# The first weights' loads and conversions between the strided and the local units, and the first matmuls in a written order

## The chip, the cores and the metric

The kernel runs on one core of a Trainium2 chip. The metric is the device time of one execution in microseconds (us); less is better. A core has a matrix engine (PE, with its weight loads PEld), a vector engine (DVE), a scalar engine (ACT), a general engine (POOL) and a sync engine (SP) that here only issues transfers. Each works through its own list of instructions in order and waits on semaphores for the others.

## The reference

```python
# q, k, v: (8 batches, 8 heads, 576 positions, 64)
rel = pos[:, None] - pos[None, :]
mask_local = (rel >= 0) & (rel < 32)                                      # heads 0 to 3
mask_strided = (rel >= 0) & (pos[None, :] % 32 == pos[:, None] % 32)      # heads 4 to 7
attn = softmax(where(mask, q @ k.T / 8, -1e9)) ; out = attn @ v
x = out.transpose(0, 2, 1, 3).reshape(4608, 512)
h = x @ w_in                    # (512, 2048), 64-bit input
return (h * cos(h)) @ w_out     # (2048, 512), 64-bit input
```

## The kernel before

The work has two phases. In the first, each of the eight batches goes through attention and then through `x @ w_in`; the hidden values go to DRAM (`h_all`). In the second, 144 tiles of 128x512 hidden values are read back, multiplied by their cosine and by `w_out`.

Attention of a batch is seven **units**: four strided ones (two for each pair of heads) and three local ones (192 positions of four heads). A unit loads its q and k and then its v, multiplies q and k into a PSUM bank (the scores), goes through a softmax (DVE: largest value, subtraction; ACT: exponential; DVE: sum, small addition, reciprocal; POOL: product with the reciprocal), is transposed (a strided unit by PE and a copy on ACT, a local one by DVE alone), and is multiplied by v. In the units of batch 0 the products of a local unit are split right away into a rounded part `x_hi` (ACT) and the rest `x_lo` (DVE); those of the strided units are collected in `x0` and split once all four are there, by ACT and POOL (`FirstOperands.split`). The tiles that batch 0 loads into are named `v`, those of the later batches `qk` and `v`.

`x @ w_in` of batch 0 is eight `FirstBlock`s, one for each 256 columns. Each has eight products of six 128x288 matmuls, handed out to seven slots. A product with the strided half of x needs `x_hi`/`x_lo` of `x0` and the first two slots of the first block (18 matmuls) need nothing else; the third slot needs the local half. The weights come as 64-bit numbers in two 512 KB transfers for each block (`land`, tile `raw`, three buffers). `to_float32` makes them 32-bit with two instructions on ACT and two on DVE, and `split` makes the two parts with one on ACT and one on POOL (tile `w`). The later blocks' conversions are handed out over the slots.

What sets the order: SP issues all loads but the constants. PE's instructions are chained in the order in which the program writes them (`in_turn`); in the prologue of the kernel before, that chain is not used and the scheduler places PE's instructions. On the other engines the scheduler orders what is ready by its own reckoning, within what `order` demands. `PROLOGUE` lists by step which units (0 to 3 strided, 4 to 6 local, of batch 0) go one stage further. After each of the first steps come a few matmuls of no use (`keep_busy`, 128x512, 31 in all), whose number is in `BUSY`; ten of them stand after the products of unit 3. The first block's weights are converted from step 6 on, the second block's after the whole prologue. The weight loads come after the loads of batch 0's seven units (`units first`).

After the prologue the loop over slots runs: a product, then the attention of the next batch (`burst`), whose scores all use one PSUM bank, `acc0`. So the scores of the next unit wait until DVE has read the last ones.

Of the kernel before, what the change touches and what calls it, by code (L numbers as in the profile page):

```python
# [13 lines left out]
F32 = mybir.dt.float32  # L14
# [8 lines left out]
B, H, S, D = 8, 8, 576, 64  # L23
# [47 lines left out]

PROLOGUE = ((0,), (1,), (2,), (3,), (0, 4), (1, 0, 5), (2, 1, 6), (3, 2), (4, 4), (3,), (5, 5), (6, 6))
BUSY = (9, 2, 2, 2, 2, 2, 2, 10)

# [8 lines left out]
def attention_cos_ffn(ctx, tc, qkl, vl, qkvs, w_in, w_out, eye, eye16, mask_l0, mask_l, mask_s, out):  # L83
# [47 lines left out]
    def with_product(begun):  # L131
        if turn is not None:
            order(begun, turn, "with this product")

    def land(cv, src):
        raw = cv.tile([P, 512, 2], I32, name="raw", bufs=3)
        load = nc.sync.dma_start(out=raw.rearrange("p n w -> p (n w)"), in_=src)
        if len(loads) == UNITS:
            order(load, loads[-1], "units first")
        return raw  # L140
# [62 lines left out]
    class Attention:  # L203
        def __init__(self, stack):
            self.plain = True
# [11 lines left out]
        def banks(self, plain, scores, transposed, products, second):  # L217
            self.plain = plain
            self.scores, self.transposed, self.products, self.second = (
                itertools.cycle(kind) for kind in (scores, transposed, products, second)  # L220
            )

        def pe(self, mm):
            self.last = mm
            return mm if self.plain else in_turn(mm)

# [4 lines left out]
        def score_bank(self, b, mask):  # L231
            if b == 0:
                bank = self.bank(self.scores)
                n, w = mask.shape[1:]
                self.pe(nc.tensor.matmul(
                    bank[:, :n * w].rearrange("p (t w) -> p t w", w=w), ident16, mask, start=True, stop=False,
                    skip_group_check=True,
                ))
# [43 lines left out]
        def local(self, b, u):  # L282
            qk, v = self.inputs(b, QKL)
            loads.append(nc.sync.dma_start(out=qk[:, :QKL], in_=qkl[b, u]))
            nc.sync.dma_start(out=v[:, :VL], in_=vl[b, u])
            q_t = qk[:, :2 * LQ].rearrange("p (h q) -> p h q", h=2)
# [5 lines left out]
            def score(t, c):  # L292
                p, j = divmod(c, 2)
                self.scored = self.pe(nc.tensor.matmul(  # L294
                    s_ps[quarter_of(c), t * KW:(t + 1) * KW], q_t[half(j), p, QB * t:QB * (t + 1)],
                    k_t[half(j), p, QB * t:QB * t + KW], start=b > 0, stop=True, skip_group_check=True,
                ))
# [10 lines left out]
            def product(m, c):  # L308
                p, j = divmod(c, 2)
                lo, hi = max(m - 1, 0), min(m + 1, LU)  # L310
                at = m * KW - QB if m else 0
                self.pe(nc.tensor.matmul(  # L312
                    a_ps[p][half(j), lo * QB:hi * QB], v_t[quarter_of(c), m], pt[quarter_of(c), at:at + (hi - lo) * QB],
# [20 lines left out]
        def strided(self, b, p, u):  # L334
            real = min(SU, NG - SU * u)
            qk, v = self.inputs(b, QS + KS)
            spare = self.spare
            loads.append(nc.sync.dma_start(out=qk[:, :QS + KS], in_=qkvs[b, p, u, :, :QS + KS]))
            nc.sync.dma_start(out=v[:, :real * D], in_=qkvs[b, p, u, :, QS + KS:QS + KS + real * D])
            q_t = qk[:, :QS].rearrange("p (t q) -> p t q", q=GB)  # L340
# [5 lines left out]
            def score(t, i):  # L346
                self.scored = self.pe(nc.tensor.matmul(
                    s_ps[half(1 - i, GB), t * GB:(t + 1) * GB], q_t[half(i), t], k_t[half(i), t],
# [14 lines left out]
            for t in range(0, SU, 2):  # L363
                self.pe(nc.tensor.transpose(  # L364
                    t_ps[:, t * GP:(t + 2) * GP], pn[:, t:t + 2].rearrange("p t k -> p (t k)"), ident
                ))
# [8 lines left out]
            def product(t, j):  # L375
                at = (t ^ 1) * GB
                self.pe(nc.tensor.matmul(  # L377
                    a_ps[half(j), t * GB:(t + 1) * GB], v_t[half(j, GB), t], pt[half(j, GB), at:at + GB], start=True,
# [237 lines left out]
    with ExitStack() as phase:  # L616
# [18 lines left out]
        acc = [(ps, f"acc{i}") for i in range(3)]  # L635
        att.banks(True, (m,), (o,), (acc[1], acc[2]), (acc[0], o))
        operands[0] = FirstOperands()
# [3 lines left out]

        def keep_busy(bank, n, after):
            for _ in range(n):
                mm = nc.tensor.matmul(
                    bank, warm, warm.unsqueeze(1).broadcast_to([P, 4, P]), start=True, stop=True
                )
                if after is not None:
                    order(mm, after, "in its place")
                after = mm
# [18 lines left out]
        att.banks(False, (acc[0],), (acc[1],), (acc[2],), (acc[1],))  # L668

# [173 lines left out]
```

## Time and profile before

| | |
|---|---|
| median of 3 runs | 884.25 us (882.93 to 885.15) |
| the profiled execution | 883.67 us |
| its span | 881.9 us |
| PE busy | 869.3 us (99%) |
| DVE, ACT, POOL busy | 562.3, 530.1, 398.2 us |
| first product of `x @ w_in` | 29.75 us into the span |
| from then on PE waits | 2.7 us in all up to 130 us |

A row of the timeline gives the start in us from the start of the span, the duration in us, engine, line, operation, what is written and read, and how many instructions the row takes together. In brackets stands how long the engine had been idle before, and what ended that. The granted clock is a share of TensorE's 2.4 GHz; 0.5 is the lower of its two levels, 1.2 GHz.

### The profile page before, as it was taken

What the parts mean: (1) busy time and instruction counts of PE and PEld (TensorE: products, weight loads), DVE (VectorE), ACT (ScalarE), POOL (GpSimd) and SP (SyncE); (2) the same over time, 40 slices, a digit from 0 to 9 for tenths busy, and PEclk for the clock granted to TensorE, in tenths of its full rate; (3) what the DMA queues carried; (4) which work ended last, traced back from release to release, by engine and by line L of the source; (5) the groups of instructions that cost most, each with busy time, mean ns of one, the idle gap of its engine ahead of it and who ended that gap; (6) DMA issues with size and microseconds to landing.
All of it is one profiled execution on the core that took longest, in us unless ns stands there. A gap on an engine that the chain in (4) does not pass through costs nothing.

```text
span 881.9 us, 21351 instructions
## 1 busy us (share of the span) xinstructions
PE 869.3 (99%) x8439; PEld 775.9 (88%) x8439; DVE 562.3 (64%) x966; ACT 530.1 (60%) x1020; POOL 398.2 (45%) x341
## 2 busy tenths in 40 slices
PE   8999999999999999999999999999999999999998
PEld 5799899999999999999999888888888888888886
DVE  5778655767576675676425666666666666666662
ACT  3776544435445463454457777777777777777772
POOL 2578974316024051151355444444444444444442
PEclk9999999999999999999999999999999999999999
DMA  9697444565556556643285434343434344444431
GB/s 333 206 294 259 141 147 158 196 220 191 195 188 234 198 196 201 197 159 122 101 278 188 135 96 144 100 145 101 144 100 141 112 129 120 128 119 121 131 109 48
DMA packets 70516, 143.83 MB, mean 163 GB/s; under 512 B 8208, under 2 KB 15632, under 8 KB 70416
## 3 DMA queue, kind: packets, MB, share of 16 engines
q1 hardware_dynamic: 69696, 142.24, 50.2%
q8 instruction: 66, 1.08, 0.5%
q14 instruction: 34, 0.28, 0.1%
q10 hardware_dynamic: 720, 0.23, 0.1%
HBM read 91.06 MB, written 51.38 MB: 162 GB/s over the span
## 4 chain that ended last, share of the span: by engine, by line
PE 52%; DMA 2%; ACT 1%; POOL 1%; DVE 0%; issue 0%; POOLq 0%; ACTq 0%
PE acc L602 44%; PE m L511 4%; PE n L511 2%; DMA both<-w_all 2%; PE o L511 1%; POOL w L160 1%; PE acc L312 0%; PE acc L377 0%; ACT w L159 0%; ACT r L585 0%; DVE r L586 0%; PE acc L294 0%; ACT r L587 0%; ACT L587 0%; PE acc L364 0%
## 5 line engine op out<-in xcount | busy, mean ns | idle before, releaser
L160 POOL TENSOR_TENSOR g_lo<-r,g_hi 128x512 fp32r<-128x512 f32 x144 | 186.3, 1294 | 205.2 <-ACT g_hi L159 201.0
L602 PE MATMUL acc<-w,g_hi 128*128 128x512 f32 x720 | 221.6, 389 | 0.0
L591 DVE TENSOR_TENSOR r<-r,h_in 128x512 f32<-128x512 f32 x144 | 151.0, 1049 | 103.9 <-ACT r L587 103.6
L602 PEld LDWEIGHTS acc<-w,g_hi 128*128 128x128 f32 x720 | 135.2, 188 | 28.1
L602 PE MATMUL acc<-w,g_lo 128*128 128x512 f32 x360 | 140.0, 389 | 0.0
L585 ACT ACTIVATE r<-h_in 128x512 int32<-128x512 f32 x144 | 91.1, 633 | 77.0 <-POOL g_lo L160 76.3
L602 PE MATMUL acc<-v,g_hi 128*128 128x512 f32 x432 | 133.0, 389 | 0.0
L587 ACT ACTIVATE r<-r,quarter 128x512 f32<-128x512 f32 x144 | 104.4, 725 | 23.1 <-DVE r L586 22.9
L586 DVE SCALAR_TENSOR_TENSOR r<-r,h_in 128x512 f32<-128x512 int32 x144 | 101.7, 707 | 22.4 <-ACT r L585 11.1
L511 PE MATMUL m<-x_hi,w 128*128 128x288 f32 x448 | 109.8, 300 | 1.9 <-DVE h L529 1.5
L511 PE MATMUL m<-x_hi,v 128*128 128x288 f32 x448 | 109.1, 298 | 1.0 <-ACT m L519 0.9
L602 PEld LDWEIGHTS acc<-v,g_hi 128*128 128x128 f32 x432 | 81.0, 188 | 16.8
L159 ACT CAST g_hi<-r 128x512 fp32r<-128x512 f32 x144 | 89.6, 623 | 2.4 <-PE acc L602 1.2
L602 PE MATMUL acc<-v,g_lo 128*128 128x512 f32 x216 | 84.0, 389 | 0.0
L511 PEld LDWEIGHTS m<-x_hi,w 128*128 128x128 f32 x448 | 78.0, 188 | 3.8 <-DVE h L529 2.2
L511 PEld LDWEIGHTS m<-x_hi,v 128*128 128x128 f32 x448 | 78.0, 188 | 2.5 <-ACT m L519 1.7
L602 PEld LDWEIGHTS acc<-w,g_lo 128*128 128x128 f32 x360 | 67.5, 188 | 14.0
L519 ACT COPY m<-m 128x288 f32<-128x288 f32 x112 | 44.5, 397 | 57.3 <-PE m L511 52.3
L511 PE MATMUL m<-x_lo,w 128*128 128x288 f32 x224 | 66.1, 295 | 0.0
L511 PE MATMUL m<-x_lo,v 128*128 128x288 f32 x224 | 66.1, 295 | 0.0
L264 POOL TENSOR_TENSOR pn_s<-e_sb,z 128x324 f32<-128x324 f32 x28 | 21.2, 756 | 93.3 <-DVE z L262 72.2
L264 POOL TENSOR_TENSOR e_sb<-e_sb,z 128x384 f32<-128x384 f32 x24 | 20.9, 872 | 92.1 <-DVE z L262 81.6
(115 smaller groups left out, 1704.5 us busy)
## 6 DMA issues: line engine op xcount, KB each, us to landing
h_all<-h SPq DMA_DIRECT2D x128, 288.0 KB, 2.7
h_in<-h_all SPq DMA_DIRECT2D x144, 256.0 KB, 2.7
out<-o SPq DMA_DIRECT2D x36, 256.0 KB, 2.4
qk<-in_qkvs SPq DMA_DIRECT2D x28, 324.0 KB, 4.0
qk<-in_qkl SPq DMA_DIRECT2D x21, 416.0 KB, 3.9
raw<-in_w_in SPq DMA_DIRECT2D x16, 512.0 KB, 4.7
raw<-in_w_out SPq DMA_DIRECT2D x16, 512.0 KB, 4.3
v<-in_vl SPq DMA_DIRECT2D x24, 224.0 KB, 3.1
```

Of the source, the lines that this page charges most:

```text
L159: with_product(nc.scalar.copy(out=hi, in_=x))
L160: nc.gpsimd.tensor_tensor(out=lo, in0=x, in1=hi.bitcast(F32), op=ALU.subtract)
L264: nc.gpsimd.tensor_tensor(out=pn, in0=e, in1=z[:, :n].unsqueeze(2).broadcast_to([P, n, w]), op=ALU.mult)
L511: in_turn(nc.tensor.matmul(bank, a[:, c * P:(c + 1) * P], y[:, c], start=first and i == 0, stop=i == len(ops) - 1, skip_group_check=True,))
L519: nc.scalar.copy(out=t, in_=self.bank[name[0]])
L585: with_product(nc.scalar.activation(out=k, in_=h, func=AF.Copy, scale=1.0 / (2.0 * math.pi), bias=0.25))
L586: nc.vector.scalar_tensor_tensor(out=r, in0=k, scalar=-2.0 * math.pi, in1=h, op0=ALU.mult, op1=ALU.add)
L587: sin = nc.scalar.activation(out=r, in_=r, func=AF.Sin, bias=quarter)
L591: nc.vector.tensor_tensor(out=r, in0=r, in1=h, op=ALU.mult)
L602: in_turn(nc.tensor.matmul(acc[t], g[:, at], w, start=(f == 0 and i == 0), stop=(f == NFC - 1 and i == 2)))
```

## The change

The weight loads of the first block are put right behind the loads of the strided units, and the loads of the local units behind those: each of the first fourteen loads of units and the first four of weights is ordered behind the last one of these. The loads of batch 1 aren't part of that chain. The conversions of both blocks are stepped through by hand in the prologue. PE's prologue is one written list: Zn stands for n matmuls of no use (27 in all), a digit for the next stage of that unit, W and V with 0 or 1 for the next step of the first and second block's weights, X for the split of `x0`, P0 and P1 for the first two slots of the first block. These now stand among the local units' products, and all of PE's prologue is chained in that order.

```diff
-PROLOGUE = ((0,), (1,), (2,), (3,), (0, 4), (1, 0, 5), (2, 1, 6), (3, 2), (4, 4), (3,), (5, 5), (6, 6))
-BUSY = (9, 2, 2, 2, 2, 2, 2, 10)
+PROLOGUE = (
+    "Z9 0 Z2 1 Z2 2 Z2 3 W0 W1 Z2 0 Z2 1 0 Z2 W0 2 1 W0 W1 4 Z1 3 2 W1 5 Z2 3 X 6 Z3 V0 V1 4 4 P0 5 5 P1 6 6"
+)
...
+    def queued(load, b):
+        if b == 0:
+            if loads:
+                order(load, loads[-1], "in turn")
+            loads.append(load)
+
     def land(cv, src):
         raw = cv.tile([P, 512, 2], I32, name="raw", bufs=3)
         load = nc.sync.dma_start(out=raw.rearrange("p n w -> p (n w)"), in_=src)
-        if len(loads) == UNITS:
-            order(load, loads[-1], "units first")
+        if loads:
+            order(load, loads[-1], "in turn")
+        if len(loads) < 2 * UNITS + 4:
+            loads.append(load)
         return raw
...
-        def pe(self, mm):
-            self.last = mm
-            return mm if self.plain else in_turn(mm)
...
         def local(self, b, u):
             qk, v = self.inputs(b, QKL)
-            loads.append(nc.sync.dma_start(out=qk[:, :QKL], in_=qkl[b, u]))
-            nc.sync.dma_start(out=v[:, :VL], in_=vl[b, u])
+            for load in (
+                nc.sync.dma_start(out=qk[:, :QKL], in_=qkl[b, u]), nc.sync.dma_start(out=v[:, :VL], in_=vl[b, u])
+            ):
+                queued(load, b)
...
-        att.banks(True, (m,), (o,), (acc[1], acc[2]), (acc[0], o))
+        att.banks((m,), (o,), (acc[1], acc[2]), (o, acc[0]))
...
-        keep_busy(spare, BUSY[0], None)
-        for k, staged in enumerate(PROLOGUE):
-            for i in staged:
-                stage(units[i])
-            if k + 2 < len(BUSY):
-                keep_busy(spare, BUSY[k + 1], att.scored)
-            if k == 6:
-                turn = att.scored
-                for i in range(2):
-                    list(input_weights(cv, 0, i))
-            if k == 9:
-                keep_busy(pools["m"].tile([P, 512], F32, name="m"), BUSY[-1], att.last)
-                turn = att.last
+        first = [FirstBlock(f) for f in range(NF)]
+        early = {kind: [input_weights(cv, f, i) for i in range(2)] for f, kind in enumerate("WV")}
+        for word in PROLOGUE.split():
+            kind, n = word[0], int(word[1:] or 0)
+            if kind == "Z":
+                for _ in range(n):
+                    in_turn(nc.tensor.matmul(
+                        spare, warm, warm.unsqueeze(1).broadcast_to([P, 4, P]), start=True, stop=True
+                    ))
+            elif kind in early:
+                next(early[kind][n])
+            elif kind == "X":
                 operands[0].split(0)
                 operands[0].split(1)
-        for i in range(2):
-            list(input_weights(cv, 1, i))
+            elif kind == "P":
+                first[0].products(n)
+            else:
+                stage(units[int(word)])
...
         for f in range(NF):
-            first = FirstBlock(f)
-            for slot in range(STEP):
-                plan[STEP * f + slot] = partial(first.products, slot)
+            for slot in range(0 if f else 2, STEP):
+                plan[STEP * f + slot] = partial(first[f].products, slot)
...
+        for i in range(2):
+            for step in early["V"][i]:
+                pass
```

The lists of instructions that result differ at three places. The first is SP's list behind the eight loads of the strided units (`in_qkvs` into `v`). `in_qkl` and `in_vl` into `v` are batch 0's local units, `raw` are weights, whatever goes into `qk` and the `v` after it is batch 1. Before:

```order
L284 DMA v_263<-in_qkl 128x832
L285 DMA v_263<-in_vl 128x448
L284 DMA v_327<-in_qkl 128x832
L285 DMA v_327<-in_vl 128x448
L284 DMA v_389<-in_qkl 128x832
L285 DMA v_389<-in_vl 128x448
L137 DMA raw_430<-in_w_in 128x1024
L137 DMA raw_441<-in_w_in 128x1024
L137 DMA raw_601<-in_w_in 128x1024
L338 DMA qk_651<-in_qkvs 128x648
```

The same place of SP's list with the change:

```order
L146 DMA raw_255<-in_w_in 128x1024
L146 DMA raw_257<-in_w_in 128x1024
L346 DMA qk_646<-in_qkvs 128x648
L347 DMA v_647<-in_qkvs 128x384
L346 DMA qk_728<-in_qkvs 128x648
L347 DMA v_729<-in_qkvs 128x320
L290 DMA qk_806<-in_qkl 128x832
L290 DMA v_807<-in_vl 128x448
L290 DMA v_325<-in_qkl 128x832
L290 DMA v_325<-in_vl 128x448
L290 DMA v_390<-in_qkl 128x832
L290 DMA v_390<-in_vl 128x448
```

The two weight loads and six loads of batch 1's first three units now stand ahead of the first local load of batch 0, which was the ninth of SP's transfers and is the seventeenth; the third local unit's loads and the second block's weights follow.

The second place is DVE's list at the softmaxes of the three local units. Before, the second one begins while the first is under way (`mx_293`, `e_sb_292` and `z_297` are the first unit's, `mx_357`, `e_sb_356` and `z_361` the second's, `mx_419` the third's):

```order
L252 TENSOR_REDUCE mx_293<-m_266 128x6
L261 TENSOR_SCALAR z_250<-z_250 128x6
L253 TENSOR_TENSOR e_sb_292<-m_266,mx_293 128x384
L262 RECIPROCAL z_250<-z_250 128x6
L260 TENSOR_REDUCE z_297<-e_sb_292 128x6
L261 TENSOR_SCALAR z_297<-z_297 128x6
L252 TENSOR_REDUCE mx_357<-m_330 128x6
L262 RECIPROCAL z_297<-z_297 128x6
L253 TENSOR_TENSOR e_sb_356<-m_330,mx_357 128x384
L302 STREAM_TRANSPOSE pt_l_302<-e_sb_292 128x384
L260 TENSOR_REDUCE z_361<-e_sb_356 128x6
L252 TENSOR_REDUCE mx_419<-m_392 128x6
```

The same place of DVE's list with the change (the first unit's instructions and the second's):

```order
L257 TENSOR_REDUCE mx_355<-m_328 128x6
L258 TENSOR_TENSOR e_sb_354<-m_328,mx_355 128x384
L265 TENSOR_REDUCE z_359<-e_sb_354 128x6
L266 TENSOR_SCALAR z_359<-z_359 128x6
L267 RECIPROCAL z_359<-z_359 128x6
L309 STREAM_TRANSPOSE pt_l_364<-e_sb_354 128x384
L257 TENSOR_REDUCE mx_420<-m_393 128x6
L258 TENSOR_TENSOR e_sb_419<-m_393,mx_420 128x384
L265 TENSOR_REDUCE z_424<-e_sb_419 128x6
L266 TENSOR_SCALAR z_424<-z_424 128x6
L267 RECIPROCAL z_424<-z_424 128x6
L309 STREAM_TRANSPOSE pt_l_429<-e_sb_419 128x384
```

Each unit's six instructions now stand together, up to its transpose, and the third unit's six follow in the same way.

The third place is DVE's list with the change, behind the last `x_lo` of the local units and up to the subtraction of batch 1's first softmax. `n_624`/`v_623` and `n_632`/`v_623` are the conversions of the second block's weights:

```order
L162 SCALAR_TENSOR_TENSOR n_624<-raw_494,n_624 128x512
L165 SCALAR_TENSOR_TENSOR v_623<-raw_494,n_624 128x512
L333 TENSOR_TENSOR x_lo_130<-acc1_589,x_hi_129 128x192
L333 TENSOR_TENSOR x_lo_130<-o_590,x_hi_129 128x192
L162 SCALAR_TENSOR_TENSOR n_632<-raw_496,n_632 128x512
L260 TENSOR_TENSOR acc0_650<-acc0_650,ms_64 128x324
L165 SCALAR_TENSOR_TENSOR v_623<-raw_496,n_632 128x512
L261 TENSOR_REDUCE mx_665<-acc0_650 128x6
L262 TENSOR_TENSOR e_sb_664<-acc0_650,mx_665 128x324
```

Before, the same stretch of DVE's list, where `n_681`/`v_680` and `o_713` are the conversions of the third block's weights, and the second block's lie ahead of it:

```order
L326 TENSOR_TENSOR x_lo_130<-acc1_567,x_hi_129 128x192
L326 TENSOR_TENSOR x_lo_130<-acc0_568,x_hi_129 128x192
L151 SCALAR_TENSOR_TENSOR n_681<-raw_638,n_681 128x512
L255 TENSOR_TENSOR acc0_655<-acc0_655,ms_64 128x324
L154 SCALAR_TENSOR_TENSOR v_680<-raw_638,n_681 128x512
L151 SCALAR_TENSOR_TENSOR o_713<-raw_640,o_713 128x512
L256 TENSOR_REDUCE mx_670<-acc0_655 128x6
L489 COPY h_631<-m_630 128x288
L154 SCALAR_TENSOR_TENSOR v_680<-raw_640,o_713 128x512
L257 TENSOR_TENSOR e_sb_669<-acc0_655,mx_670 128x324
```

In this stretch the second block's four conversions take the place of the third block's; with the change the third block's four stand between the subtractions of batch 1's first and second softmax, twelve instructions apart from one subtraction to the next, where before there were seven.

## Rows read from the trace of the kernel before

**Rows 1.** The page's first part: busy time of each engine in us, share of the span, instructions.

```profile
PE 869.3 (99%) x8439; PEld 775.9 (88%) x8439; DVE 562.3 (64%) x966; ACT 530.1 (60%) x1020; POOL 398.2 (45%) x341
```

**Rows 2.** Waits of PE between 30 and 130 us: who waited for whom, us in total, times, longest.

```profile
PE acc L242 <- DVE x_lo L326: 1.2, 1, 1.2
PE n L511 <- ACT n L519: 1.1, 1, 1.1
```

**Rows 3.** The timeline of PE: matmuls of no use (L644), the first product of `x @ w_in` (L482 at 29.75), batch 1's scores (L242, L347, L294) and the products after them. The row at 34.69 is the first product with the local half, the one at 39.60 the first of the second block.

```profile
24.90 2.88 PE L644 MATMUL m<-warm 128*128 128x512 bf16 x10
...
29.75 0.40 PE L482 MATMUL m<-x_hi,w 128*128 128x288 f32 x1
...
34.69 0.40 PE L482 MATMUL m<-x_hi,w 128*128 128x288 f32 x1
...
38.88 0.80 PE L347 MATMUL acc<-qk 64*54 64x54 f32 x20
39.60 0.40 PE L482 MATMUL m<-x_hi,w 128*128 128x288 f32 x1
...
43.80 0.88 PE L294 MATMUL acc<-qk 64*32 64x64 f32 x48
```

**Rows 4.** The timeline of SP: when the first local load, the first of three weight loads and the first load of batch 1 were issued.

```profile
6.33 0.43 SPq L284 DMA_DIRECT2D v<-in_qkl  x1
...
9.73 2.47 SPq L137 DMA_DIRECT2D raw<-in_w_in  x3
12.50 0.33 SPq L338 DMA_DIRECT2D qk<-in_qkvs  x1
```

**Rows 5.** Transfers by issue, each row from the stretch in which one of those three was issued: count, KB, us from issue to landing.

```profile
v<-in_qkl SPq DMA_DIRECT2D x1, 416.0 KB, 5.5
...
raw<-in_w_in SPq DMA_DIRECT2D x1, 512.0 KB, 8.3
...
qk<-in_qkvs SPq DMA_DIRECT2D x1, 324.0 KB, 8.8
```

**Rows 6.** Transfers by issue between 0 and 70 us, for the sizes of the other loads (q and k of a strided unit of batch 0; v of a strided unit with six and with five groups; v of a local unit).

```profile
v<-in_vl SPq DMA_DIRECT2D x6, 224.0 KB, 5.9
...
v<-in_qkvs SPq DMA_DIRECT2D x4, 324.0 KB, 4.1
...
v<-in_qkvs SPq DMA_DIRECT2D x4, 192.0 KB, 4.1
v<-in_qkvs SPq DMA_DIRECT2D x4, 160.0 KB, 4.3
```

**Rows 7.** Two stretches from the start of the span: PE, PEld, DVE, ACT and POOL busy us (instructions), granted clock, share of the transfer engines, GB/s.

```profile
0.00:11.83 11.83, 10.32 (x111) 5.09 (x111) 5.20 (x16) 2.70 (x4) 3.12 (x11) 1.00 0.86 270
0.00:18.50 18.50, 16.92 (x269) 9.69 (x271) 9.36 (x29) 5.22 (x10) 6.07 (x15) 1.00 0.92 321
```

**Rows 8.** The timeline of DVE, ACT and POOL: the softmax of the first local unit and its transpose.

```profile
13.53 0.56 DVE L252 TENSOR_REDUCE mx<-m 128x6 f32<-128x384 f32 x1 [0.56 <-PE m L294]
...
14.19 0.56 DVE L253 TENSOR_TENSOR e_sb<-m,mx 128x384 f32<-128x384 f32 x1
...
14.78 0.52 ACT L258 ACTIVATE e_sb<-e_sb 128x384 f32<-128x384 f32 x1 [1.31 <-DVE e_sb L253]
...
15.34 0.55 DVE L260 TENSOR_REDUCE z<-e_sb 128x6 f32<-128x384 f32 x1 [0.49 <-ACT e_sb L258]
...
15.92 0.17 DVE L261 TENSOR_SCALAR z<-z 128x6 f32<-128x6 f32 x1
...
17.37 0.18 DVE L262 RECIPROCAL z<-z 128x6 f32<-128x6 f32 x1
...
17.70 0.83 POOL L264 TENSOR_TENSOR e_sb<-e_sb,z 128x384 f32<-128x384 f32 x1 [1.98 <-DVE z L262]
...
18.56 0.58 DVE L302 STREAM_TRANSPOSE pt_l<-e_sb 128x384 f32<-128x384 f32 x1 [0.44 <-POOL e_sb L264]
```

**Rows 9.** The timeline of POOL and DVE at the third local unit: a weight's second part on POOL, the small addition of the softmax on DVE.

```profile
22.87 1.28 POOL L160 TENSOR_TENSOR w<-v,w 128x512 fp32r<-128x512 f32 x1 [0.38 <-ACT w L159]
23.02 1.16 DVE L261 TENSOR_SCALAR z<-z 128x6 f32<-128x6 f32 x1
```

**Rows 10.** Two stretches, columns as in rows 7: the idle time of PE, and the time after it.

```profile
21.20:22.50 1.30, 0.00 (x2) 0.00 (x0) 1.30 (x4) 1.30 (x4) 0.83 (x1) 1.00 0.82 310
22.50:26.00 3.50, 3.50 (x64) 2.66 (x64) 3.47 (x8) 2.79 (x8) 2.11 (x2) 0.52 0.52 181
```

**Rows 11.** The timeline of ACT and DVE: an `x_lo` of a local unit (L326), two weight conversions in a row on ACT (L146, L150), a conversion on DVE (L151), and the subtractions of batch 1's first and second softmax (L257).

```profile
31.06 0.25 DVE L326 TENSOR_TENSOR x_lo<-acc,x_hi 128x96 fp32r<-128x96 f32 x1
...
34.16 0.63 ACT L146 ACTIVATE o<-raw 128x512 int32<-128x512 uint32 x1
34.32 0.69 DVE L151 SCALAR_TENSOR_TENSOR n<-raw,n 128x512 int32<-128x512 int32 x1 [0.73 <-ACT raw L150]
...
34.72 0.66 ACT L150 ACTIVATE raw<-raw 128x512 f32<-128x512 f32 x1
34.92 0.50 DVE L255 TENSOR_TENSOR acc<-acc,ms 128x324 f32<-128x324 f32 x1
...
37.88 0.48 DVE L257 TENSOR_TENSOR e_sb<-acc,mx 128x324 f32<-128x324 f32 x1
...
41.28 0.49 DVE L257 TENSOR_TENSOR e_sb<-acc,mx 128x324 f32<-128x324 f32 x1
```

More of the change, by code (lines that the diff above doesn't have):

```diff
@@ L204, in __init__ @@
         def __init__(self, stack):
-            self.plain = True
             self.ld, self.wk = (
@@ L215, in __init__, with banks @@
             self.kept, self.spare, self.x = None, None, {}
-        def banks(self, plain, scores, transposed, products, second):
-            self.plain = plain
+        def banks(self, scores, transposed, products, second):
             self.scores, self.transposed, self.products, self.second = (
@@ L234, in score_bank @@
                 n, w = mask.shape[1:]
-                self.pe(nc.tensor.matmul(
+                in_turn(nc.tensor.matmul(
                     bank[:, :n * w].rearrange("p (t w) -> p t w", w=w), ident16, mask, start=True, stop=False,
@@ L293, in score @@
                 p, j = divmod(c, 2)
-                self.scored = self.pe(nc.tensor.matmul(
+                in_turn(nc.tensor.matmul(
                     s_ps[quarter_of(c), t * KW:(t + 1) * KW], q_t[half(j), p, QB * t:QB * (t + 1)],
@@ L311, in product @@
                 at = m * KW - QB if m else 0
-                self.pe(nc.tensor.matmul(
+                in_turn(nc.tensor.matmul(
                     a_ps[p][half(j), lo * QB:hi * QB], v_t[quarter_of(c), m], pt[quarter_of(c), at:at + (hi - lo) * QB],
@@ L337, in strided @@
             spare = self.spare
-            loads.append(nc.sync.dma_start(out=qk[:, :QS + KS], in_=qkvs[b, p, u, :, :QS + KS]))
-            nc.sync.dma_start(out=v[:, :real * D], in_=qkvs[b, p, u, :, QS + KS:QS + KS + real * D])
+            for load in (
+                nc.sync.dma_start(out=qk[:, :QS + KS], in_=qkvs[b, p, u, :, :QS + KS]),
+                nc.sync.dma_start(out=v[:, :real * D], in_=qkvs[b, p, u, :, QS + KS:QS + KS + real * D]),
+            ):
+                queued(load, b)
             q_t = qk[:, :QS].rearrange("p (t q) -> p t q", q=GB)
@@ L346, in score @@
             def score(t, i):
-                self.scored = self.pe(nc.tensor.matmul(
+                in_turn(nc.tensor.matmul(
                     s_ps[half(1 - i, GB), t * GB:(t + 1) * GB], q_t[half(i), t], k_t[half(i), t],
@@ L363, in strided @@
             for t in range(0, SU, 2):
-                self.pe(nc.tensor.transpose(
+                in_turn(nc.tensor.transpose(
                     t_ps[:, t * GP:(t + 2) * GP], pn[:, t:t + 2].rearrange("p t k -> p (t k)"), ident
@@ L376, in product @@
                 at = (t ^ 1) * GB
-                self.pe(nc.tensor.matmul(
+                in_turn(nc.tensor.matmul(
                     a_ps[half(j), t * GB:(t + 1) * GB], v_t[half(j, GB), t], pt[half(j, GB), at:at + GB], start=True,
@@ L640, in attention_cos_ffn @@
         spare = ps.tile([P, 512], F32, name="acc0")
[L642 to L649, printed above, removed]
-        keep_busy(spare, BUSY[0], None)
-        for k, staged in enumerate(PROLOGUE):
-            for i in staged:
-                stage(units[i])
-            if k + 2 < len(BUSY):
-                keep_busy(spare, BUSY[k + 1], att.scored)
-            if k == 6:
-                turn = att.scored
-                for i in range(2):
-                    list(input_weights(cv, 0, i))
-            if k == 9:
-                keep_busy(pools["m"].tile([P, 512], F32, name="m"), BUSY[-1], att.last)
-                turn = att.last
+        first = [FirstBlock(f) for f in range(NF)]
[4 more added lines that the diff above has]
+                for _ in range(n):
+                    in_turn(nc.tensor.matmul(
+                        spare, warm, warm.unsqueeze(1).broadcast_to([P, 4, P]), start=True, stop=True
[3 more added lines that the diff above has]
+            elif kind == "X":
                 operands[0].split(0)
                 operands[0].split(1)
-        for i in range(2):
-            list(input_weights(cv, 1, i))
-        att.banks(False, (acc[0],), (acc[1],), (acc[2],), (acc[1],))
+            elif kind == "P":
+                first[0].products(n)
+            else:
+                stage(units[int(word)])
+        att.banks((acc[0],), (acc[1],), (acc[2],), (acc[1],))
         begun = np.interp(range(UNITS, B * UNITS + 3), [k for k, _ in KNOTS], [at for _, at in KNOTS])
```

## The prediction

> **What bounds the kernel now.** I read the busy times first: PE works for 99% of the span [rows 1]. Then its waits: from 30 to 130 us they are a couple of us [rows 2]. So once products follow one another, the end of the kernel moves with PE, and what the prologue gains or loses shows at the end one for one. No later stretch gives back time, since PE hardly waits there. What counts is how late PE is at fixed marks behind the prologue. In the timeline of PE these are [rows 3]: first product at 29.75, first product with the local half at 34.69, batch 1's second scores at 38.88, second block at 39.60, third scores at 43.80. Then I read what feeds those marks: SP's transfers, the local softmaxes, and the conversions on ACT and DVE.
>
> **What the change takes off PE's path.** The first two slots' 18 matmuls start at 29.75 and run at full clock in some 2.4 us; they now stand between the local units' products. The ten matmuls of no use behind unit 3's products (2.88 us [rows 3]) are gone. The first block's weights no longer compete with the local softmaxes. All of this gains only if PE isn't waiting there for something that now comes later, which is the next point.
>
> **The local units' loads.** In SP's list the first local q and k was the ninth transfer and is now the seventeenth: two weight loads and, outside the new chain, six loads of batch 1 stand ahead of it. In before it was issued at 6.33 and landed 5.5 us later, at 11.8 [rows 4, 5]. With the change there lie ahead of it four strided units, 4x324 + 2x192 + 2x160 = 2000 KB, 1024 KB of weights, and for batch 1 the same kinds of loads, 324 + 192 + 324 + 160 + 416 + 224 = 1640 KB [rows 5, 6]. With its own 416 KB that makes 5080 KB. When does so much land? In before, the 4432 KB up to the first weight load (2000, three local units of 640, and 512) were in at 9.73 + 8.3 = 18.0, and the 5780 KB up to batch 1's first q and k at 12.50 + 8.8 = 21.3 [rows 4, 5]; between these, 5080 KB come at 19.6. From below: at 11.83, 270 GB/s had moved 3.19 MB, 0.72 MB more than the 2.47 MB in order up to the tile that landed then. 5.20 + 0.72 MB had been moved by 18.5 (321 GB/s) [rows 7]. I take **19.2**, nearer the landing times, because as many transfers are under way there.
>
> **The local softmaxes.** DVE's list now has each local unit's six instructions in one piece, and the transpose at the end waits for POOL, so the second softmax can't begin before the first is through. One of them, without queueing, is [rows 8]: from 13.53 to the end of the small addition at 16.09 is 2.56; the reciprocal comes 0.03 later; from its start to the end of the transpose, 17.37 to 19.14, is 1.77. That is 4.36 us, and three in a row are 13.1. The first unit's scores take some 0.9 us (the 0.88 of the row at 43.80 [rows 3]). So the third unit is transposed at 19.2 + 0.9 + 13.1 = **33.2**. Loads of the second and third unit land within some 4 us of the first and are hidden behind this chain. So is the first block's conversion, ahead of it.
>
> Here PE still keeps up: `x0` can be split only once ACT has done the second unit's exponential (about 26.3), and POOL's two `x_lo` of it end near 31, so P0 runs from some 29.7 and the third unit's products end near 35.
>
> **The conversions behind them.** What PE meets next is a list that DVE and ACT have to work off. The subtraction of batch 1's first softmax must end before the second scores can use `acc0`. Ahead of it DVE now has the second block's four conversions, which in before were spread between 27 and 32 us. My sum: the last four `x_lo` and the casts between them need about 1.2 us (0.25 for one [rows 11], alternating with ACT), so ACT turns to the conversions at 34.4. Up to the one that DVE needs last (`n_632`) it has five conversions and a cast, which follow one another every 0.56 us (34.16 to 34.72 [rows 11]), and two small casts of 0.2: 3.9 us with a handover, to 38.3. Then DVE has the conversion (0.6, as from 34.32 to 34.92), the mask, another conversion, the reduction and the subtraction, 2.7 us in all: 41.0. In before that subtraction ended at 38.36 [rows 11] and PE came to the scores just then, 38.88. So PE is **2.2 us late** here (41.05 to 38.88).
>
> From there to the next subtraction DVE has twelve instructions where it had seven. Seven took 38.36 to 41.77, 3.4 us [rows 11]; four conversions more (0.6 each, less one copy shared) make 5.5, so that subtraction ends at 46.5. In before PE had 2.0 us to spare at this place (41.77 to 43.80); now it would come at 43.80 + 2.2 = 46.0 and waits **0.5 us** more. After that the two lists have the same work between marks, and no stall is left to add.
>
> **The clock.** PE is idle from about 16 to 19 us and again from about 26 to 29.7. In before, after 1.3 us of idle time and the many small matmuls around it, the granted clock was 0.52 for 3.5 us [rows 10], that is 1.2 GHz. I add 0.3 us for the first scores at that level; the rest of a low stretch is hidden, since DVE and ACT set the marks. The Trainium skill ("TensorE: Matmul & The Clock Gate", section on HAM oscillation) says that a wait for transfers between short pieces of matmuls brings the array to half its clock, and that the price is paid at each such wait; the trace agrees with 0.52 after the idle time, and by that rule both new waits would be followed by a low stretch, which would leave the sum as it is unless the second reaches past 37 us (rival 4).
>
> **Sum.** 2.2 + 0.5 + 0.3 = 3.0 us. My chains put almost nothing between engines, where rows show up to 0.1 us for each handover; for some of these I add 0.3. From the profiled execution's 883.67 that gives 887.0. It lay 0.6 under the median, so for the median I forecast 884.25 + 3.3 = **887.5**. A measurement of this kernel can tell 0.3% from no change, that is 2.65 us: the bounds are 881.6 and 886.9.
>
> A price that I leave out of the sum: in before, the small addition on DVE took 1.16 us instead of 0.17 while POOL made a weight's second part in 1.28, and ended with it [rows 8, 9]. The third softmax's addition falls at about 31.2, just behind POOL's `x_lo` of `x0`; if they meet, it costs up to 1.0. The Trainium skill ("SBUF — State Buffer", section on the two separate sides) calls the port pair of these two engines an exclusive lock, held for a whole instruction; the trace agrees with the 1.16, and by it the sum would be 4.3 instead of 3.3 if they meet.
>
> **The rivals.**
> 1. The forecast: local tiles land between 18.5 and 19.6, and the chains follow. Each us of landing moves the marks by one, so with the meeting on POOL at the upper end it gives 886.3 to 888.9. Chance 0.52.
> 2. The tiles land sooner but still behind batch 1's. Their load can't be issued before the eighth transfer ahead of it, a weight load, has landed at about 12.1 (2512 KB against the 2416 at 11.8); if it then takes 5.5 us as before, it lands at 17.6, and 3.3 - 1.6 leaves 886.0. For it: SP waits no longer than that. Against it: 8.3 to 8.8 us in the stretch when the engines are full [rows 5]. Chance 0.21.
> 3. Not slower: batch 1's loads cost the local ones nothing, because transfers under way share the engines. Then only 3440 KB count ahead and with them, which by the rows between 2416 at 11.8 and 4432 at 18.0 is 15.0; 4.2 us earlier than in the sum, that is 0.9 us faster than before, 883.4. The point from which it decides: a landing before 15.9. Against it: landing times in before follow the order of issue. Should the softmaxes overlap better too, it passes the bound of faster. Chance 0.14.
> 4. Much slower: the clock is still at 1.2 GHz when the 30 products of the first block's rest begin near 37 us. They take 4.2 us at full clock (34.69 to 38.88 [rows 3]) and would take 8.4; PE would come to the second scores at 45.4 instead of 41.0, and, less the 0.5 that it then no longer waits, the time is about 891. For it: the long idle times. Against it: PE has work from 29.7 on, and the low stretch of before lasted 3.5 us with PE busy. Chance 0.13.
>
> **How the numbers follow.** Slower by over 0.3% holds where the forecast's case lies above 886.9, some 0.43 of its 0.52, with rival 4's 0.13 and a little of rival 2: 0.58. Faster by over 0.3% is half of rival 3, 0.07. The rest, 0.35, is within. The range goes from 883.6 (rival 3's upper half and all of rival 2) to 890.6 (all but the larger part of rival 4), and leaves out less than 0.2.
>
> **What would show it.** In the profile after: the first local scores of batch 0 near 19 us, with PE idle for some 3 us ahead of them; three local transposes on DVE about 4.3 us apart, the last ending near 33; batch 1's second scores near 41 (before 38.9), waiting for DVE's subtraction; the second block near 41.8 (39.6) and the third scores near 46.5 (43.8); the granted clock low somewhere between 20 and 36. Local scores before 16 us would make the prediction wrong, and so would a second block near 39.6 in spite of late scores, which would mean that DVE and ACT work off their lists faster than I sum.

## The result, and the profile after

| | before | after |
|---|---|---|
| median, us | 884.35 (4 runs) | 889.5 (889.14 to 890.85, 4 runs) |
| profiled execution, us (its span) | 883.67 (881.9) | 889.18 (887.4) |

The ratio is 1.0063, with a 95% interval of 1.0045 to 1.008: the change costs 5.15 us by the medians, where 3.3 had been forecast. Of the profile I read the same marks on PE as before. Timeline of PE after; L301 at 18.64 are the first local scores, L492 the products of `x @ w_in`, L357 at 45.44 batch 1's second scores, L492 at 46.73 the second block, L301 at 51.43 the third scores:

```profile
18.64 0.87 PE L301 MATMUL m<-v 64*32 64x64 f32 x48 [1.95 <-DMA v<-in_qkl]
...
29.02 0.40 PE L492 MATMUL m<-x_lo,w 128*128 128x288 f32 x1 [1.48 <-POOL x_lo L171]
...
35.13 0.40 PE L492 MATMUL m<-x_hi,w 128*128 128x288 f32 x1
...
37.49 0.29 PE L492 MATMUL m<-x_hi,w 128*128 128x288 f32 x1
42.26 0.61 PE L492 MATMUL m<-x_hi,w 128*128 128x288 f32 x1 [4.48 <-DVE h L499]
...
45.44 1.36 PE L357 MATMUL acc<-qk 64*54 64x54 f32 x20
46.73 0.61 PE L492 MATMUL m<-x_hi,w 128*128 128x288 f32 x1
...
51.43 0.87 PE L301 MATMUL acc<-qk 64*32 64x64 f32 x48
```

Against [rows 3] the first product with the local half is only 0.44 us late (35.13 to 34.69). The second scores are 6.56 late, the second block 7.13, the third scores 7.63. So nearly all of the loss arises between 37.8 and 47.6 us, in two pieces: a stop of 4.48 us, and products that then take longer: the twelve up to the second scores need 3.18 us (42.26 to 45.44), where the run with the clock kept, below, has 1.80. The releaser named is DVE's copy of a finished bank into `h` (L499): the next product needs that bank. What held the copy, in the timelines of DVE, ACT and SP:

```profile
35.48 0.69 DVE L165 SCALAR_TENSOR_TENSOR v<-raw,n 128x512 int32<-128x512 int32 x1
...
39.51 0.49 DVE L262 TENSOR_TENSOR e_sb<-acc,mx 128x324 f32<-128x324 f32 x1
41.15 0.70 DVE L162 SCALAR_TENSOR_TENSOR o<-raw,o 128x512 int32<-128x512 int32 x1 [1.15 <-ACT raw L161]
41.76 0.45 DVE L499 COPY h<-m 128x288 f32<-128x288 f32 x1
```

```profile
39.93 0.62 ACT L157 ACTIVATE o<-raw 128x512 int32<-128x512 uint32 x1 [2.58 <-DMA raw<-in_w_in]
```

```profile
17.07 19.50 SPq L146 DMA_DIRECT2D raw<-in_w_in  x4
36.66 0.38 SPq L346 DMA_DIRECT2D qk<-in_qkvs  x1
```

and, between 10 and 45 us, what SP waited for (us in total, times, longest):

```profile
SPq L146 <- DVE v L165: 18.5, 4, 12.6
```

Read from the bottom: SP's fourth weight load in that row was issued at its end, 36.57, because it needed one of the three `raw` buffers: SP's weight loads waited 18.5 us in all for the conversions that read them, and the last of these to end before the issue is the second block's first, 35.48 to 36.17. ACT got the load 3.4 us later and worked from 39.93, DVE's conversion waited for ACT until 41.15, and the copy, one place behind it in DVE's list, ended at 42.21. DVE stood idle for 1.15 us with a copy behind it that was ready. In stretches of 2 us (columns as in [rows 7]):

```profile
17.00:19.00 2.00, 0.36 (x24) 0.36 (x28) 1.38 (x2) 0.89 (x4) 1.10 (x1) 1.00 1.06 417
27.00:29.00 2.00, 0.55 (x19) 0.29 (x9) 1.32 (x3) 0.23 (x1) 2.00 (x3) 1.00 0.00 0
39.00:41.00 2.00, 0.00 (x0) 0.00 (x0) 0.97 (x3) 1.07 (x2) 0.00 (x0) 1.00 0.86 313
41.00:43.00 2.00, 0.74 (x3) 0.74 (x4) 1.85 (x4) 2.00 (x6) 1.28 (x1) 0.51 0.35 143
43.00:45.00 2.00, 2.00 (x10) 2.00 (x10) 1.67 (x5) 0.70 (x3) 0.15 (x1) 0.50 0.55 152
45.00:47.00 2.00, 2.00 (x24) 1.62 (x23) 0.62 (x2) 1.70 (x4) 2.00 (x3) 0.50 1.15 299
47.00:49.00 2.00, 2.00 (x13) 2.00 (x14) 1.93 (x4) 0.00 (x0) 1.07 (x1) 0.78 0.75 248
```

The granted clock was 1.00 through the two early waits and fell to 0.50 (1.2 GHz) after the stop. By a later mark, the 21st store of an `h`, PE is 7.7 us late (issued at 127.61, before at 119.90); at the end of the span it is 5.5. The difference comes back where before itself waits: its listed waits of PE between 130 and 500 us add up to 3.1 us, those of after to 1.6. Not every kernel gets as much back: of the ten below, the five with the second block early gain 1.5 to 2.1 us between this mark and the end of the span, the other five from 0.3 us down to a loss of 0.9. Why they differ is open.

### The profile page after: what moved, and what is told of

It reads as the page before. It is cut to its first block, busy times and chain, and to the rows that moved or that the text cites. A ratio compares the mean times of both kernels' runs of the same rounds, so it can differ in the third digit from the quotient of the medians.

```text
span 887.4 us, 21340 instructions
## 1 busy us (share of the span) xinstructions
PE 869.7 (98%) x8435; PEld 776.9 (88%) x8435; DVE 567.4 (64%) x966; ACT 530.2 (60%) x1020; POOL 398.3 (45%) x341
## 4 chain that ended last, share of the span: by engine, by line
PE 91%; DVE 3%; DMA 3%; POOL 2%; ACT 1%; issue 1%; SPq 0%; POOLq 0%; ACTq 0%; DVEq 0%
PE acc L612 44%; PE m L521 19%; PE n L521 10%; PE m L492 5%; PE o L521 5%; PE acc L319 2%; PE acc L301 2%; PE acc L387 2%; PE acc L357 1%; DMA raw<-in_w_in 1%; PE acc L374 1%; DMA v<-in_qkl 1%; POOL x_lo L171 1%; DMA v<-in_qkvs 0%; POOL e_sb L269 0%
## 5 line engine op out<-in xcount | busy, mean ns | idle before, releaser
L521 PE MATMUL m<-x_hi,w 128*128 128x288 f32 x448 | 109.8, 300 | 2.1 <-DVE h L539 1.6
L492 PE MATMUL m<-x_hi,w 128*128 128x288 f32 x256 | 57.5, 308 | 4.5 <-DVE h L499 4.5
```

The source lines that it names most:

```text
L492: in_turn(nc.tensor.matmul(self.banks[i, j], a[:, c * P:(c + 1) * P], y[:, c], start=k == 0 and m == 0, stop=k == 1 and m == len(ops) - 1, ...
L521: in_turn(nc.tensor.matmul(bank, a[:, c * P:(c + 1) * P], y[:, c], start=first and i == 0, stop=i == len(ops) - 1, skip_group_check=True,))
```

## Experiments

"The mark at 125 us" in the expectations is that 21st store. Medians are of 4 to 12 runs, ratios are against runs of before on the same chip; none of the kernels leaves work out. Mark and scores are read in one profiled execution of each kernel, whose time can lie up to 2.6 us from the median and has a column of its own. The intervals of after, the copy first, the clock kept and batch 1's loads behind all overlap, so no difference in time among these four is shown.

| run | median, us | ratio, 95% interval | profiled, us | mark, us | second scores at |
|---|---|---|---|---|---|
| after | 889.5 | 1.0063 (1.0045 to 1.008) | 889.18 | +7.7 | 45.44 |
| copy first | 888.5 | 1.0053 (1.0041 to 1.0065) | 888.5 | +5.1 | 42.87 |
| clock kept | 889.64 | 1.0075 (1.0062 to 1.0088) | 889.65 | +6.2 | 45.12 |
| batch 1's loads behind | 889.01 | 1.0062 (1.0047 to 1.0076) | 891.08 | +7.6 | 45.36 |
| both (first and third) | 885.8 | 1.0032 (1.002 to 1.0044) | 887.61 | +3.3 | 42.02 |
| second block early | 886.4 | 1.003 (1.002 to 1.0039) | 884.85 | +2.7 | 41.69 |
| local loads first | 892.83 | 1.011 (1.0092 to 1.0128) | 895.39 | +10.8 | 48.77 |
| local first, second block early | 889.02 | 1.0058 (1.0045 to 1.0071) | 887.92 | +6.4 | 45.03 |
| second block early, copy first | 885.15 | 1.0025 (1.0014 to 1.0036) | 883.73 | +1.9 | 40.79 |
| all three | 883.97 | 1.0002 (0.9993 to 1.0011) | 882.54 | +0.4 | 39.12 |
| all three, weight in the gap | 882.24 | 0.9992 (0.9982 to 1.0002) | 881.68 | -0.4 | 38.55 |

**The copy first.** `copies` collects DVE's copies into `h`; conversions written later are placed behind the latest.

```diff
-        nc.vector.scalar_tensor_tensor(
+        first_stt = nc.vector.scalar_tensor_tensor(
...
+        if copies:
+            order(first_stt, copies[-1], "copy first")
...
-                        nc.vector.tensor_copy(out=h[:, TH * j:TH * (j + 1)], in_=self.banks[i, j])
+                        copies.append(nc.vector.tensor_copy(out=h[:, TH * j:TH * (j + 1)], in_=self.banks[i, j]))
```

> The changed kernel, with one thing moved: on DVE the copy that frees the product bank (h) stands ahead of the conversion of the third block's second weights. Theory A (the wait of 4.5 us at 37.7 comes of DVE's list: the copy stands behind a conversion whose weights land only at 39.9): the wait goes; PE comes to the second scores at 40.1, where DVE's subtraction has just ended (40.0), to the third scores at 46.4 instead of 51.4; no low clock after 41; time 885 (884 to 886.5). Theory B (the prediction's: the late local tiles and DVE's pile of conversions hold PE at the scores in any case): the wait moves to the second and third scores, time 888 or more.

Timelines of PE and DVE:

```profile
40.49 0.40 PE L494 MATMUL m<-x_hi,w 128*128 128x288 f32 x1 [2.64 <-DVE h L501]
...
42.87 1.36 PE L359 MATMUL acc<-qk 64*54 64x54 f32 x20
```

```profile
39.58 0.49 DVE L264 TENSOR_TENSOR e_sb<-acc,mx 128x324 f32<-128x324 f32 x1
39.99 0.45 DVE L501 COPY h<-m 128x288 f32<-128x288 f32 x1
41.36 0.69 DVE L162 SCALAR_TENSOR_TENSOR o<-raw,o 128x512 int32<-128x512 int32 x1 [0.92 <-ACT raw L161]
```

The wait for the late load is off the copy's path: 1.8 us of the stop are gone and 2.6 of the mark. What remains, 2.64 us, is the list itself: the copy now stands right behind the subtraction, which ends at 40.07. Behind that stop the clock fell again (0.63 and 0.52 from 41 to 45 us), which theory A had ruled out. At the end of the span only 0.7 us is left of the 2.6, so the time is the one that theory B named, while the trace shows that the wait for the late load was real and had a second bound right behind it.

**The clock kept.** Twenty products of no use fill the stop.

```diff
+            if self.f == 0 and slot == 5:
+                idle = ps.tile([P, 512], F32, name="acc2")
+                for _ in range(20):
+                    in_turn(nc.tensor.matmul(
+                        idle, warm, warm.unsqueeze(1).broadcast_to([P, 4, P]), start=True, stop=True
+                    ))
```

> The changed kernel, with 20 matmuls of no use (0.215 us each, 4.3 us) written in where PE waits 4.5 us for the copy. DVE's list is as in the changed kernel, so the wait stays, but PE is busy in it. Theory A with the clock as a cost of its own (30 products and the second scores at 1.2 GHz took 0.24 us each where 0.13 is usual): second scores near 43.9 instead of 45.4, third near 49 instead of 51.4, time 887. If the low clock costs nothing because DVE sets the marks anyway: 889.5.

```profile
38.67 4.49 PE L486 MATMUL acc<-warm 128*128 128x512 bf16 x20
43.32 0.40 PE L498 MATMUL m<-x_hi,w 128*128 128x288 f32 x1 [0.16 <-DVE h L505]
...
45.12 0.80 PE L357 MATMUL acc<-qk 64*54 64x54 f32 x20
...
50.04 0.87 PE L301 MATMUL acc<-qk 64*32 64x64 f32 x48
```

From the restart to the third scores it is 6.72 us (43.32 to 50.04) where after has 9.17 (42.26 to 51.43): the low clock costs 2.45 us there. In this execution an earlier low stretch, 0.50 behind the first local scores, came with a local chain and a copy that ended 1.06 later; the mark gains 1.5, and by the end (a span of 887.9) nothing is left of it. The price of the clock is shown at the marks; the median, that of after, doesn't show it.

**Batch 1's loads behind the local ones.**

```diff
+            firsts.append(load)
+        elif b == 1:
+            order(load, firsts[-1], "behind the first batch")
```

> The changed kernel, with the first loads of batch 1 ordered behind the local loads of batch 0. Both theories: the first local tile lands 1640 KB earlier, near 14.5 instead of 18.6, the third transpose ends near 28.4 instead of 32.5, and the first product with the local half comes near 31 instead of 35.1. Theory A: the order on DVE is the same, so the 4.5 us wait and the low clock stay and are 4 us earlier; time 885.4. Rival C (the local tiles' landing isn't on the path, the weights' ring of three buffers is): the mark at 35 moves, the third scores stay near 51, time 889.

Time and third scores (51.36) are the rival's; the 31 us that both theories gave the first product with the local half didn't come:

```profile
36.32 0.40 PE L495 MATMUL m<-x_hi,w 128*128 128x288 f32 x1
...
42.18 0.61 PE L495 MATMUL m<-x_hi,w 128*128 128x288 f32 x1 [3.21 <-DVE h L502]
```

The first local scores ran at 16.59, 2 us earlier than in after, and the last local transpose ended at 31.52, 0.96 earlier. But PE, at a clock of 0.50 from 28 to 34, came to the product in the first row 1.19 later than in after (35.13), and the copy was still behind the late load (a stop of 3.21 us): the mark stayed. The profiled execution is the slowest of the six; whether the others had the low stretch isn't known. Together with the copy first:

> Batch 1's loads behind the local ones, and the copy first on DVE. Theory A: both gains, third scores near 42.3 (before: 43.8), time 881.5 (880 to 883), faster than the kernel before. Theory B: DVE's conversions take the gain of the second part; time 885.

The stop is 1.75 us, and the median of 885.8 is near theory B's 885. On the same chip the copy alone gave 888.5 and the loads alone 889.01, so either of them is worth 2 to 3 us when the other is there (by the medians 3.2 for the copy and 2.7 for the loads, by the ratios 2.7 and 1.9), and alone at most about 1 against after: each hides the other. The profiled execution, 1.8 us above the median, also lost time to the clock, after waits of 1.44 and 1.92 us:

```profile
25.00:27.00 2.00, 0.40 (x1) 0.19 (x1) 0.96 (x4) 0.96 (x2) 1.48 (x2) 0.90 0.74 275
27.00:29.00 2.00, 1.24 (x5) 1.24 (x6) 1.32 (x3) 0.91 (x3) 2.00 (x2) 0.50 0.06 22
29.00:31.00 2.00, 2.00 (x20) 1.72 (x22) 0.92 (x4) 0.04 (x1) 0.91 (x2) 0.50 0.00 0
```

**The second block early.** The words of the second block (`V`: load, conversion, split) move ahead in PE's prologue, and with them DVE's conversions and the release of the `raw` buffers.

```diff
-... X 6 Z3 V0 V1 4 4 P0 5 5 P1 6 6
+... X 6 V0 V1 Z3 V0 V1 4 4 P0 V0 V1 5 5 P1 6 6
```

> The second block's first conversions stand inside the third local softmax instead of behind it, so the raw buffers come free near 30 us instead of 36 and the load that DVE's fifth conversion needs lands near 35 instead of 40. Theory A (PE stops because the copy that frees its bank stands on DVE behind a conversion whose load is late): the third transposed tile comes 1 us later, but the copy ends near 40 instead of 42.2, the stop of 4.5 us falls to about 2, the mark at 125 us goes from +7.6 to +5, and the time to 887 to 888. Theory B (DVE's list is simply full, whatever the order): the four conversions taken from behind are paid ahead, the stop moves to the third unit's products, and the time stays at 889.5.

```profile
34.06 0.30 PE L319 MATMUL acc<-pt_l,v 32*64 32x32 f32 x4 [1.14 <-issue]
...
39.90 0.40 PE L492 MATMUL m<-x_hi,w 128*128 128x288 f32 x1 [0.87 <-ACT h L501]
...
41.69 0.80 PE L357 MATMUL acc<-qk 64*54 64x54 f32 x20
```

```profile
28.82 0.69 DVE L162 SCALAR_TENSOR_TENSOR n<-raw,n 128x512 int32<-128x512 int32 x1
...
39.24 0.69 DVE L162 SCALAR_TENSOR_TENSOR o<-raw,o 128x512 int32<-128x512 int32 x1
```

The second block's first conversion stands at 28.82 (34.74 in after), the `o` conversion waits for nothing, the stop is 0.87 us, and no low stretch follows. The wait of 1.14 ahead of the third unit's products is new and has no releaser by the profile; DVE's last local transpose ends at 33.66, 1.2 later than in after. The mark moves by 5.0 where theory A said 2.6, and the median, 886.4, is under its range. Theory B's time falls, though part of the conversions is paid ahead, as it said. The edit takes two things off the copy's path at once, the late load and the second block's conversions; the run with the copy first parts them, 1.84 us of the stop for the load and 2.64 for the list.

**The order of loads undone.** Loads as in before (strided, local, weights, batch 1), PE's order as in after:

```diff
-... Z2 3 W0 W1 Z2 0 Z2 1 0 Z2 W0 2 1 W0 W1 4 Z1 3 2 W1 5 Z2 3 X 6 Z3 ...
+... Z2 3 Z2 0 Z2 1 0 Z2 2 1 4 Z1 3 2 5 Z2 3 X 6 W0 W1 W0 W1 W0 W1 Z3 ...
```

> The loads stand in the order of before: strided units, local units, weights, batch 1; TensorE's prologue stays in the written order. DVE's list then has the three local softmaxes interleaved and the first block's conversions behind them. Theory A (the loss comes from the order of loads and what DVE's list makes of it): local scores near 13 us, the time is that of before or a little under it, 882.5 to 885. Theory C (the written order of PE itself costs, since the first two slots' products wait for x_lo and for the banks): 887 or more in spite of early local tiles.

```profile
16.52 0.87 PE L301 MATMUL m<-v 64*32 64x64 f32 x48
...
24.44 0.64 PE L301 MATMUL m<-v 64*32 64x64 f32 x14 [2.22 <-issue]
...
29.61 0.61 PE L492 MATMUL m<-x_hi,w 128*128 128x288 f32 x1 [1.69 <-ACT w L170]
```

Theory A missed, by 8 us, and theory C's 887 or more holds. The profiled execution lay 2.56 us above the median. Two bounds of the written order show in it. The local scores don't run near 13 but at 16.52 without any wait listed, since PE's list has the strided units' products ahead; no run with PE's written order had them before 16.27. And the first two slots' products must run before the second and third units' products, so weights that are ready late (`w` at 29.6) hold the local half too: 39.57 for its first product. A stop of 3.37 us for the copy stays besides. So the new order of PE without the new loads loses most; the new loads without the new order weren't run. With the second block early added:

> Local loads first and the second block's conversions inside the local softmaxes. Theory A: the copy is no longer behind a late load and local tiles are early, so PE has no stop over 1 us after its first product; 880.5 to 883. Theory B or C: no better than the kernel with the local loads first alone.

It is 3.8 us better than without, and still 5.4 behind before, so neither expectation held. From 24 to 50 us PE's listed waits are four for weights, 4.96 us in all, and one of 0.94 for a copy:

```profile
PE m L492 <- ACT w L170: 3.6, 2, 2.8
PE m L492 <- POOL w L171: 1.3, 2, 0.8
```

**The copy first, with the second block early.** In addition to both edits the third block's first conversion is written three slots later.

```diff
-                at = 7 * n + 7 * i // 2 - 13
+                at = max(7 * n + 7 * i // 2 - 13, 4)
```

> The second block's conversions stand inside the third local softmax, as before, and the third block's first conversions stand behind the copy that frees the bank. Theory A (what is left of the stop, 0.9 us, is the place of the copies behind the third block's conversions): no stop over 0.4 us between the first product with the local half and the second scores, mark at 125 us near +2 (was +2.8), 885.5 to 886. Theory B (the conversions that move behind the copy are missed at the third block): 886.4 or more.

No stop is left there, and the second scores run at 40.79. The median is 0.35 under theory A's range. Batch 1's loads moved back as well:

> As the run with the copy first, and batch 1's six loads stand behind the local ones. Theory A (once the copy no longer decides, the local landing does, as the prediction had it): local scores near 16.5, third transpose some 1.3 us earlier, 883.5 to 884.5. Theory D (the granted clock falls in the wait for x_lo, as it did with batch 1's loads moved back alone, and takes the gain): 885.5 or more, with the clock near 0.5 for some 6 us from 27 on.

PE's timeline without that last edit, and with it:

```profile
19.11 0.88 PE L303 MATMUL m<-v 64*32 64x64 f32 x48 [2.41 <-DMA v<-in_qkl]
...
40.79 0.80 PE L359 MATMUL acc<-qk 64*54 64x54 f32 x20
```

```profile
16.34 0.88 PE L306 MATMUL m<-v 64*32 64x64 f32 x48
...
39.12 0.80 PE L362 MATMUL acc<-qk 64*54 64x54 f32 x20
```

Now that nothing else is late, the landing counts: scores 2.77 us earlier bring the second scores 1.67 forward and the median from 885.15 to 883.97, no different from before. Of the missing 1.1 us a part is DVE's, which converts a first-block weight until 18.5 ahead of the first local reduction. That conversion was moved into the softmax's gap:

```diff
-... W0 2 1 W0 W1 4 Z1 3 2 W1 5 Z2 3 X 6 ...
+... W0 2 1 W0 4 Z1 3 2 W1 5 W1 Z2 3 X 6 ...
```

> As the run with all three, and the first block's second weight is converted behind the first local subtraction on DVE instead of ahead of the first local reduction, for which DVE was busy until 18.4 while the scores ended at 17.2. Theory A (the chain of local softmaxes on DVE now sets the end of the prologue): the first reduction begins near 17.2, the third transpose comes some 1 us earlier, 882.7 to 883.3, 0.5 to 1.2 below the run with all three and just under the kernel before. Theory E (PE is then held by POOL's x_lo or by weights that come later, and the later stretch takes back what is left): 884.

```profile
17.35 0.56 DVE L262 TENSOR_REDUCE mx<-m 128x6 f32<-128x384 f32 x1 [1.91 <-PE m L306]
...
31.07 0.58 DVE L314 STREAM_TRANSPOSE pt_l<-e_sb 128x384 f32<-128x384 f32 x1 [0.38 <-POOL e_sb L274]
```

The reduction begins 1.04 us earlier than in the run with all three (18.39), the last transpose 0.58 (31.65) and the second scores 0.57, and the median is 882.24, the lowest here and 0.46 under theory A's range. The interval against before includes 1, and it overlaps with that of the run with all three: a gain over either isn't shown.

## Why the prediction was right about the sign and short of the size

**The local tile's landing: right.** 18.6 measured, 19.2 forecast (18.5 to 19.6). That each us of landing moves the marks by one was wrong for this kernel (2 us gave nothing while the copy was late and the clock low) and became 0.6 once the copy was out of the way.

**The three softmaxes one after another: right.** DVE's local transposes begin at 23.39, 27.64 and 31.90, 4.25 apart (forecast 4.36); the last ends at 32.5, not 33.2. The price left out for POOL's and DVE's meeting was rightly left out: POOL's `x_lo` ended at 30.36, and the small addition behind it took 0.17.

**What PE meets next: the step that failed.** The prediction had PE come to the second scores and wait there 2.2 us for the subtraction. That subtraction ended at 40.0 (forecast 41.0), so DVE's list was summed well enough. But PE never came so far: it stopped twelve products earlier, at the one that needs the bank of the copy. The prediction followed the conversions only for what DVE would read and not for the bank copies standing in the same list, nor for the buffers that they release. The chain of late conversion, `raw` buffer, load, conversion and copy is shown by the run with the copy first, where 1.84 us of the stop go with it. The other 2.64 are DVE's list, which the prediction had summed; but it holds up PE twelve products ahead of the scores, and the prediction let those twelve run meanwhile. The run with the second block early takes both away, and 5.0 us of the mark with them. Forecast for the waits at the second and third scores were 2.2 and 0.5; the stop measures 4.48.

**The clock: mis-sized.** Forecast 0.3; measured 2.45 at the marks. It fell after the stop, not after the two idle times that the prediction named. The Trainium skill ("TensorE: Matmul & The Clock Gate", section on HAM oscillation) has the price paid at each wait between short pieces of matmuls, in a kernel whose waits are about 3 to 5 us. The trace agrees with it at the stop of 4.48 us; the two early waits of 1.95 and 1.48 us, shorter than those, passed at 1.00.

**"No later stretch gives back time": wrong.** The 0.44 at the first product with the local half, 4.48 of stop, 2.45 of low clock and 0.26 for products that don't follow one another across the stop (the 30 take 2.65 + 1.80 at full clock, in before 4.19) are the 7.63 of the third scores. 2.2 us came back by the end, 1.5 of them as listed waits that before has between 130 and 500 us and after hasn't. That is why the total, 5.15, lies within the range while the terms were further off: with the 7.7 of the mark it would have been 891.4 (883.67 + 7.7), above the range. That the size came out within it is luck.

**The rivals.** The second (17.6) and the third (15.0) fall by the landing at 18.6: the load was issued at 11.88, much as the second had it, but took 6.7 us and not 5.5. Where the tile was early, PE's order let the scores run at 16.27 at the earliest, so that the third's 15.0 could not have counted in full. The fourth's low clock came, but behind the stop: in the first block's rest ahead of it the clock was full.

## What to carry to other kernels

When work on an in-order engine moves, follow every instruction that stands behind it, the small copies that free a bank first, and ask of each conversion which buffer it gives back and which load is waiting for that buffer. Edits that gate the same place hide each other: alone they were worth at most about 1 us each, and 2 to 3 once the other was in. A wait that the profile counts as small in a later stretch can be slack: a delay ahead of it cost up to 2.2 us less at the end than at the mark where it is read, but in half of the runs here it didn't.

## What the runs showed of the hardware

The length of a wait didn't decide whether the clock fell. PE's waits of 1.95 us (after, ahead of the local scores), 2.33 (second block early, at the same place) and 1.94 (all three, for `x_lo`) were followed by 1.00; 1.30 in before [rows 10], and 2.41 in the run below, by about 0.5. Windows of the run with the second block early and the copy first, behind its wait that ended at 19.11:

```profile
19.00:21.00 2.00, 1.89 (x60) 1.56 (x62) 0.84 (x2) 0.66 (x2) 1.27 (x1) 0.89 1.05 395
21.00:23.00 2.00, 2.00 (x45) 1.57 (x45) 1.19 (x4) 1.15 (x3) 0.01 (x1) 0.50 1.03 415
```

That stretch cost nothing behind it: the last local transpose is 0.23 later than in the run with the second block early alone (33.31 to 33.08), as the landing is (19.11 to 18.88). What decides whether the clock falls is open.

PE also stopped within one group of matmuls with no releaser: after 34 of the third unit's 48 local scores, for 0.94 us in after, 2.22 in the run with the local loads first and 1.94 in the last run:

```profile
24.00 0.42 PE L306 MATMUL m<-v 64*32 64x64 f32 x14 [1.94 <-issue]
```

The place in the program is the same each time and the length is not. Nor does the length follow the transfers: the share of the transfer engines over these three stops was 0.49, 0.18 and 1.02. The cause is open; whether PE's own instructions came late wasn't tried.
